# Sparse attention and top-2 experts on one core: how the early expert jobs fetch their rows, how strided values are loaded, and what paces the indirect transfers

## The chip, the cores and the metric

The kernel runs on one core of a Trainium2 chip. The metric is the device time of one execution in microseconds (us); less is better. The time of a kernel is the median over its runs.

The core has five engines that run at the same time and meet through semaphores: TensorE (PE in the profile), which multiplies matrices into PSUM and also transposes; VectorE (DVE); ScalarE (ACT); GpSimd (POOL), which here mostly issues indirect transfers (gathers and scatters whose row numbers lie in SBUF); and SyncE (SP), which issues the plain transfers. Each engine works through its instructions strictly in the order in which they were written.

## The reference

Attention over 8 batches, 8 heads, 576 positions and 64 values per head. Four heads see only the last 32 positions (local), four see only positions with the same remainder by 32 (strided). Its output is x, 4608 tokens of 512 values, and feeds a mixture of 8 experts of which each token uses 2.

```python
def _attn_ref(q, k, v):
    B, H, S, D = q.shape                      # 8, 8, 576, 64
    scores = (1.0 / np.sqrt(D)) * np.matmul(q, k.transpose(0, 1, 3, 2))
    rel = pos[:, None] - pos[None, :]
    mask_local = (rel >= 0) & (rel < 32)
    mask_strided = (rel >= 0) & (pos[None, :] % 32 == pos[:, None] % 32)
    ...                                       # softmax over the masked scores
    return np.matmul(attn, v)

def _moe_ref(x, w_gate, w_noise, noise, w1, w2):   # x: 4608 x 512
    noisy_logits = x @ w_gate + np.log1p(np.exp(x @ w_noise)) * noise
    top2 = np.argpartition(-noisy_logits, 2, axis=1)[:, :2]
    ...                                       # top2_w: softmax over the two
    for e in range(8):
        for k in range(2):
            mask = top2[:, k] == e
            h = np.maximum(x[mask] @ w1[e], 0.0)          # 512 -> 1024
            out[mask] += top2_w[mask, k, None] * (h @ w2[e])  # 1024 -> 512
```

## The kernel before, in words

**Attention.** The work is cut into 32 units: 8 batches times four pairs of heads, strided and local in turn. `loads` (L435) brings a unit's k, q and v through SP two units ahead, `prep` (L476) transposes k and q on PE, `products` (L523) makes the masked scores, `item` (L562) does softmax and values, and `finish` (L648) stores the unit's columns of x to the DRAM tensor `x_dram` and keeps a transposed copy `xT` for the gate. The values of a strided unit go to the tile `v_s`, which keeps 65 numbers per position (64 values and a one), so the load writes 64 values at a time, one line of 256 B each.

**Routing.** After the four units of a batch, `route` (L706) computes the gate for its 576 tokens, ranks the two experts of each, and scatters 12 x 96 entries (token, weight, row of `x_dram`) into `tab`, one list per expert: 12 indirect transfers on POOL per batch (L817).

**Experts.** An expert's list is worked in jobs of two or three blocks of 128 tokens. `SUBS` (L63) gives each job its place in the list and the number `hb` of batches after which those places are certain to be filled. Seven jobs of experts 0 to 2 have `hb` below 8, 16 blocks in all: these early jobs run between the attention units. All others wait for batch 8. For a job, `gather` (L901) loads the entries of the list through SP (L908), makes row numbers on POOL (L935, L954) and gathers the rows of x: `x_dram` holds four 128-column pieces of a token as four rows that lie 576 rows apart, and each block takes four gathers of 128 rows of 512 B (L946), the row numbers being offset by quarter (`qoff`), so that a 32x32 block transposition by DVE (L970, in `transposes`, L960) puts the columns onto the partitions. ACT then rounds the result to a high part (L974) and DVE subtracts it to a low part (L976). `layer1` (L988) and `layer2` (L1049) multiply high and low parts on PE, three products for one, at L1002 and L1064. `previous` (L1037) gathers the rows of the output so far (L1042); they are added on DVE (L1089) and scattered back (L1094). The output is filled with zeros by 12 plain transfers (L1148) of 384 rows each, and `previous` waits for those that cover its batches.

**Order.** Nothing of the order is left to the hardware. Every piece of work is a `Piece` with an engine (ANY is ACT or DVE), an estimated duration, a rank and its dependencies; `issue_all` (L291) is a list scheduler that keeps estimated clocks of all engines and of the wire, takes the piece that can start first (among those within 120 ns the one of lowest rank), and writes its instructions in that order. What the code sets around the change:

- A plain transfer is counted with its bytes times `wires` over 270 bytes per ns; a piece that needs a transfer's data may start `far` ns after its planned landing. A transfer marked `bulk` (a zero fill) is taken only when at most 1500 ns of wire time are planned ahead, and not before its `t0`.
- Expert work on PE is let in by a balance (`owed`) of about one to one with attention, and holds at most four PSUM banks while attention lasts.
- A piece that reads PSUM and writes a ring slot forces the PSUM writer to come after the slot was handed out. So the PE products of a block's layer 2 stand behind the start of `previous` for that block.
- An indirect transfer on POOL is also made to wait for a step of DVE or ACT that is planned to have ended 200 ns before it (the latest of either), so that it doesn't run ahead of its plan:

```python
behind = [x for m in marks.values() for x in m[-40:] if x[0].end + 200 <= t]
if behind:
    x = max(behind, key=lambda x: x[0].end)
    if x[0].end > paced[0]:
        ...   # each transfer y gets: tc.add_manual_dep(y.ins, x[1].ins.name, ...)
paced[0] = t
```

The functions that the diff touches follow, with the profile's line numbers.

Of the kernel before, what the change touches and what calls it, by code (L numbers as in the profile page):

```python
# [22 lines left out]
def kernel(  # L23
# [135 lines left out]
    v_s = [keep.tile([GP, 2, NJ, D + 1], F32, name=f"v_s{i}") for i in range(2)]  # L159
# [131 lines left out]
    def issue_all(expert_banks, t_start):  # L291
# [43 lines left out]
        while ready:  # L335
# [79 lines left out]
    for name, shape, dtype, depth in (  # L415
            ("raw", [LP, 2, LJ, D], F32, 2), ("ord", [LP, LJ, 2, D], F32, 1),
            ("ks", [GP, 2, NJ, D], F32, 1), ("qs", [GP, 2, NJ, D], F32, 1),
            ("mx", [128, 5], F32, 3), ("ex", [128, 5, KW], F32, 2), ("aT", [128, 5, 128], F32, 2),
            ("rs", [128, 6], F32, 2),
            ("xT", [128, S], F32, 6),  # L420
# [14 lines left out]
    def loads(u, rank):  # L435
# [21 lines left out]
        if local:  # L457
# [4 lines left out]
                             [[D, QB], [QB * D, 2 * NBL], [1, D]], 589824)], True)  # L462
# [185 lines left out]
    def finish(u, xo, rank):  # L648
# [3 lines left out]
        base = (b * 4 + d) * S * 128  # L652
# [4 lines left out]
        if local:  # L657
            store(lambda t: t[:, :4, :, :].rearrange("r g h d -> r g (h d)"), 0,
                  [[128, 128], [128 * 128, 4], [1, 128]], 262144)
            store(lambda t: t[:QB, 4, :, :].rearrange("r h d -> r (h d)"), 512 * 128, [[128, QB], [1, 128]], 32768)  # L660
        else:
            for half in range(2):

                store(lambda t, half=half: t[64 * half:64 * half + 64, :4, :, :].rearrange(
                    "r (m g) h d -> r m (g h d)", m=2),
                      (QB + 2 * half) * 128, [[NJ * 128, QB], [4 * 128, 2], [1, 256]], 131072)
            store(lambda t: t[:QB, 4, :, :].rearrange("r h d -> r (h d)"), 0, [[128, QB], [1, 128]], 32768)
# [579 lines left out]
```

## Time and profile before

| | us |
|---|---|
| median of 3 runs | 1115.05 (1113.36 to 1119.16) |
| the profiled execution | 1116.99 |
| its span, first to last instruction | 1115.2 |
| PE busy in the span | 1066.9 (96%) |
| POOL busy | 606.9 (54%) |
| DVE busy | 615.2 (55%) |
| ACT busy | 429.9 (39%) |

The profile is that of one execution. It names instructions by line of the kernel, engine and operation, with `out<-in` tiles; PEld is the weight load of PE, which overlaps the products, and SPq, POOLq are transfers as their engine issues them. PEclk is the share of the full TensorE clock that was granted. A busy PE is not a PE at its peak: at half the clock it is busy twice as long. The attention units fill the span to about 315 us; from about 366 us on the kernel does expert jobs alone.

### The profile page before, as it was taken

What the parts mean: (1) busy time and instruction counts of PE and PEld (TensorE: products, weight loads), DVE (VectorE), ACT (ScalarE), POOL (GpSimd) and SP (SyncE); (2) the same over time, 40 slices, a digit from 0 to 9 for tenths busy, and PEclk for the clock granted to TensorE, in tenths of its full rate; (3) what the DMA queues carried; (4) which work ended last, traced back from release to release, by engine and by line L of the source; (5) the groups of instructions that cost most, each with busy time, mean ns of one, the idle gap of its engine ahead of it and who ended that gap; (6) DMA issues with size and microseconds to landing.
All of it is one profiled execution on the core that took longest, in us unless ns stands there. A gap on an engine that the chain in (4) does not pass through costs nothing.

```text
span 1115.2 us, 23354 instructions
## 1 busy us (share of the span) xinstructions
PE 1066.9 (96%) x8581; PEld 940.5 (84%) x8581; DVE 615.2 (55%) x1618; ACT 429.9 (39%) x1103; POOL 606.9 (54%) x789
## 2 busy tenths in 40 slices
PE   7988889899998999999999999999999999999993
PEld 5767669788887989898998989898988898898992
DVE  4787976867764434655673455345534643473430
ACT  5687966856633211423341223123311321151220
POOL 1044464566656765656666555655646474656510
PEclk6898979999999999999999999999999999999997
DMA  9698997879775532445553226324522452253210
GB/s 189 165 204 199 229 219 172 184 199 248 198 203 102 161 88 72 135 145 148 176 165 117 83 78 195 95 61 115 174 74 68 126 164 69 77 161 92 73 42 22
DMA packets 184886, 153.03 MB, mean 137 GB/s; under 512 B 74695, under 2 KB 155079, under 8 KB 184752
## 3 DMA queue, kind: packets, MB, share of 16 engines
q1 hardware_dynamic: 159664, 92.40, 34.3%
q0 software_dynamic: 25088, 58.87, 17.7%
q8 instruction: 81, 1.33, 0.5%
q14 instruction: 53, 0.43, 0.1%
HBM read 112.86 MB, written 39.39 MB: 137 GB/s over the span
## 4 chain that ended last, share of the span: by engine, by line
PE 66%; DMA 0%; DVE 0%; issue 0%; POOL 0%; POOLq 0%; DVEq 0%
PE bankE L1064 5%; PE bankF L1064 5%; PE bankH L1064 4%; PE bankD L1064 4%; PE bankB L1064 4%; PE bankB L1002 4%; PE bankD L1002 4%; PE bankF L1002 4%; PE bankC L1002 4%; PE bankH L1002 4%; PE bankE L1002 4%; PE bankA L1002 4%; PE bankG L1002 4%; PE bankC L1064 4%; PE bankA L1064 4%; PE bankG L1064 3%
## 5 line engine op out<-in xcount | busy, mean ns | idle before, releaser
L946 POOL DMA_INDIRECT xg<-x_dram,gxx x304 | 307.4, 1011 | 145.0 <-issue 69.9
L1094 POOL DMA_INDIRECT out_dram<-prev,tabt x80 | 83.3, 1041 | 105.0 <-DVE prev L1089 38.5
L817 POOL DMA_INDIRECT tab<-ent,addr x96 | 93.4, 973 | 62.5 <-issue 10.3
L1042 POOL DMA_INDIRECT prev<-out_dram,gix x80 | 78.3, 979 | 80.5 <-DMA out_dram<-prev,tabt 29.4
L970 DVE STREAM_TRANSPOSE xr<-xg 128x512 f32<-128x512 f32 (+1 forms) x80 | 84.3, 1054 | 20.2 <-DMA xg<-x_dram,gxx 18.5
L974 ACT CAST xhi<-xr 128x512 fp32r<-128x512 f32 (+1 forms) x80 | 47.7, 596 | 95.7 <-DVE xr L970 92.7
L976 DVE TENSOR_TENSOR xlo<-xr,xhi 128x512 fp32r<-128x512 f32 (+1 forms) x80 | 53.2, 665 | 26.4 <-ACT xhi L974 25.0
L888 DVE TENSOR_TENSOR w1lo<-wraw,w1hi 128x512 fp32r<-128x512 f32 x80 | 55.0, 690 | 6.6 <-ACT w1hi L887 4.3
L887 ACT CAST w2hi<-wraw 128x512 fp32r<-128x512 f32 x80 | 46.7, 617 | 29.4 <-DMA wraw<-in_moe_w_dram 8.4
L888 DVE TENSOR_TENSOR w2lo<-wraw,w2hi 128x512 fp32r<-128x512 f32 x80 | 52.1, 682 | 3.9 <-ACT w2hi L887 3.3
L887 ACT CAST w1hi<-wraw 128x512 fp32r<-128x512 f32 x80 | 48.6, 614 | 2.5 <-DMA wraw<-in_moe_w_dram 2.4
L1002 PE MATMUL bankB<-xhi,w1hi 128*128 128x256 f32 (+3 forms) x128 | 39.4, 308 | 2.6 <-ACT xhi L974 2.6
L1002 PE MATMUL bankG<-xhi,w1hi 128*128 128x256 f32 (+3 forms) x136 | 41.1, 302 | 0.0
L1002 PE MATMUL bankG<-xhi,w1lo 128*128 128x256 f32 (+3 forms) x136 | 40.7, 300 | 0.0
L1002 PE MATMUL bankG<-xlo,w1hi 128*128 128x256 f32 (+3 forms) x136 | 40.5, 298 | 0.0
L1002 PE MATMUL bankE<-xhi,w1hi 128*128 128x256 f32 (+3 forms) x132 | 39.9, 302 | 0.0
L1002 PE MATMUL bankD<-xhi,w1hi 128*128 128x256 f32 (+3 forms) x132 | 39.8, 302 | 0.0
L1002 PE MATMUL bankC<-xhi,w1hi 128*128 128x256 f32 (+3 forms) x132 | 39.7, 301 | 0.0
L1002 PE MATMUL bankB<-xlo,w1hi 128*128 128x256 f32 (+3 forms) x128 | 38.8, 303 | 0.7 <-DVE xlo L976 0.7
L1002 PE MATMUL bankD<-xhi,w1lo 128*128 128x256 f32 (+3 forms) x132 | 39.4, 298 | 0.0
L1002 PE MATMUL bankC<-xhi,w1lo 128*128 128x256 f32 (+3 forms) x132 | 39.4, 298 | 0.0
L1002 PE MATMUL bankE<-xhi,w1lo 128*128 128x256 f32 (+3 forms) x132 | 39.4, 298 | 0.0
(614 smaller groups left out, 3474.3 us busy)
## 6 DMA issues: line engine op xcount, KB each, us to landing
wraw<-in_moe_w_dram SPq DMA_DIRECT2D x160, 256.0 KB
out_dram<-zeros SPq DMA_DIRECT2D x12, 768.0 KB
xg<-x_dram,gxx POOLq DMA_INDIRECT x304
ks<-in_k_dram SPq DMA_DIRECT2D x15, 320.0 KB
qs<-in_q_dram SPq DMA_DIRECT2D x15, 320.0 KB
v_s<-in_v_dram SPq DMA_DIRECT2D x30, 160.0 KB
raw<-in_k_dram SPq DMA_DIRECT2D x16, 288.0 KB
v_l<-in_v_dram SPq DMA_DIRECT2D x16, 288.0 KB
```

Source lines behind the costliest of these rows:

```text
L817: st = nc.gpsimd.indirect_dma_start(out=tab, out_offset=bass.IndirectOffsetOnAxis(ap=s["addr"].t[:, t, kk:kk + 1], axis=0), in_=s["ent"].t ...
L887: Piece("ACT", act(512) + 30, lambda o: nc.scalar.copy(hi.t, raw.t), rank, read=[raw], alloc=[hi], expert=True)
L888: Piece("DVE", dve(512), lambda o: nc.vector.tensor_tensor(lo.t, raw.t, hi.t.bitcast(F32), ALU.subtract), rank, read=[raw, hi], alloc=[lo] ...
L946: dma(lambda o, i=i, g=g, xg=xg: nc.gpsimd.indirect_dma_start(out=xg.t[:, g, :], out_offset=None, in_=x_dram[:4 * known, :], in_offset=bas ...
L970: Piece("DVE", dve(4 * rows), lambda o, xg=xg, xr=xr, ng=ng, rows=rows: nc.vector.transpose(xr.t[:, :, :rows].rearrange("p c (g i) -> p g ...
L974: Piece("ACT", act(4 * rows), lambda o, xr=xr, rows=rows, cols=cols: nc.scalar.copy(xh.t[:, :, cols], xr.t[:, :, :rows]), rank, read=[xr], ...
L976: Piece("DVE", dve(4 * rows), lambda o, xr=xr, rows=rows, cols=cols: nc.vector.tensor_tensor(xl.t[:, :, cols], xr.t[:, :, :rows], xh.t[:, ...
L1002: nc.tensor.matmul(ps.t[:, :width], a.t[:, 128 * d:128 * d + 128], c.t[:, d, :width], start=(m == 0), stop=(m == len(todo) - 1))
L1042: dma(lambda o: nc.gpsimd.indirect_dma_start(out=pv.t[:rows, :], out_offset=None, in_=out[:known, :], in_offset=bass.IndirectOffsetOnAxis( ...
L1064: nc.tensor.matmul(ps.t, HT[n, f][p[0]].t[:, cols], W2[n][f][p[1]].t, start=(m == 0), stop=(m == len(todo) - 1))
L1094: st = nc.gpsimd.indirect_dma_start(out=out[:known, :], out_offset=bass.IndirectOffsetOnAxis(ap=tb.t[:rows, i, 0:1], axis=0), in_=pv.t[:ro ...
```

## The change

Five things change.

1. **Pacing of indirect transfers.** An indirect transfer on POOL now waits for the latest DVE step that is planned to have ended 200 ns earlier and later than the transfer before it; only if there is none, for such a step of ACT.
2. **List loads.** The plan starts a list load 4000 ns (`far`) after the planned landing of the scatters that it needs, not at once.
3. **Strided values.** A strided unit's values come in two loads (one per head) of 2 KB lines into a new tile `vraw` (one buffer), and ACT or DVE copies each into `v_s`. The plan's cost of loads changes with it: factor 1.65 in place of 1.45 on 256 B lines, 1.2 now on the 1.5 KB lines of local k and q, and local values counted with their true 294,912 B in place of twice as much.
4. **Rows of x.** `x_dram` is laid out by token: the four pieces of a token follow each other, 2 KB in one line. The stores of `finish` and the row numbers follow. An early job then gathers a block with one indirect transfer of 128 whole rows, by the same row numbers that `previous` uses, without the second list load and its row numbers; PE transposes the block in four 128x128 steps into one PSUM bank, from which ACT and DVE take high and low parts. Jobs with `hb` = 8 gather as before, in four, and are transposed on DVE.
5. **Zero fills and room.** The planned starts of the zero fills become 26, 36, 46, 56, 66 and then 111, 121 ... 171 us, from 50, 68 ... 248 us. `xT` has 5 buffers, not 6.

```diff
-    v_s = [keep.tile([GP, 2, NJ, D + 1], F32, name=f"v_s{i}") for i in range(2)]
+    v_s = [keep.tile([G, 2, NJ, D + 1], F32, name=f"v_s{i}") for i in range(2)]
...
-    nc.gpsimd.iota(xrow, pattern=[[4 * S, B], [TB, T]], base=0, channel_multiplier=1)
+    nc.gpsimd.iota(xrow, pattern=[[4 * TB, NTOK // TB]], base=0, channel_multiplier=4)
...
-        nc.vector.memset(qoff[32 * i:32 * i + 32, :], float(i * S))
+        nc.vector.memset(qoff[32 * i:32 * i + 32, :], float(i))
...
             if e == "POOL" and o.lat:
-                behind = [x for m in marks.values() for x in m[-40:] if x[0].end + 200 <= t]
-                if behind:
-                    x = max(behind, key=lambda x: x[0].end)
-                    if x[0].end > paced[0]:
+                for engine in ("DVE", "ACT"):
+                    behind = [x for x in marks[engine][-40:] if paced[0] < x[0].end <= t - 200]
+                    if behind:
+                        x = max(behind, key=lambda x: x[0].end)
                         for y in last if isinstance(last, list) else [last]:
                             tc.add_manual_dep(y.ins, x[1].ins.name, mybir.DependencyInfo(
                                 mybir.DependencyClass.Sync, mybir.DependencyReason.DATA), reason="in its time")
+                        break
                 paced[0] = t
...
-            ("xT", [128, S], F32, 6),
+            ("xT", [128, S], F32, 5),
...
-                    nbytes, rank, wires={D: 1.45, 4 * D: 1.2}.get(dims[-1][1], 1.0),
+                    nbytes, rank, wires={D: 1.65, LJ * D: 1.2}.get(dims[-1][1], 1.0),
...
-                             [[D, QB], [QB * D, 2 * NBL], [1, D]], 589824)], True)
+                             [[D, QB], [QB * D, 2 * NBL], [1, D]], 294912)], True)
...
-            put("v", R["v_s"].new(),
-                [(lambda t, h=h: t[:rows, h, :, :D], v, base + h * S * D, [[NJ * D, rows], [D, NJ], [1, D]], 2048 * rows)
-                 for h in range(2)], True)
+            slot = res["v"] = R["v_s"].new()
+            for h in range(2):
+                put(f"v{h}raw", R["vraw"].new(), [(lambda t: t[:rows].rearrange("p j d -> p (j d)"), v, base + h * S * D,
+                                                   [[NJ * D, rows], [1, NJ * D]], 2048 * rows)], True)
+                def spread(o, h=h, raw=res[f"v{h}raw"]):
+                    copy(o.e, slot.t[:G, h, :, :D], raw.t[:G])
+                Piece("ANY", {"ACT": act(NJ * D), "DVE": 75 + 0.52 * NJ * D}, spread, rank, read=[res[f"v{h}raw"]],
+                      **{"write" if h else "alloc": [slot]})
...
-        base = (b * 4 + d) * S * 128
+        base = b * S * DM + d * 128
...
-                    "r (m g) h d -> r m (g h d)", m=2),
-                      (QB + 2 * half) * 128, [[NJ * 128, QB], [4 * 128, 2], [1, 256]], 131072)
+                    "r (m g) h d -> r m g (h d)", m=2),
+                      (QB + 2 * half) * DM, [[NJ * DM, QB], [4 * DM, 2], [DM, 2], [1, 128]], 131072)
...
+            whole = hb < B
+            tb, gi = R["tabt"].new(), R["gix"].new()
+            tx, gx = (None, None) if whole else (R["tabx"].new(), R["gxx"].new())
...
-                dma(load, bytes_, rank if hb == B else 20 * NP * (hb - 1) + 10 * NP, after=known_tab[hb], expert=True, **how)
+                dma(load, bytes_, rank if hb == B else 20 * NP * (hb - 1) + 10 * NP, after=known_tab[hb], expert=True,
+                    far=4000, **how)
...
+            for i in range(nb) if whole else ():
+                xg = R["xg"].new()
+                dma(lambda o, i=i, xg=xg: nc.gpsimd.indirect_dma_start(
+                    out=xg.t.rearrange("p g c -> p (g c)"), out_offset=None,
+                    in_=x_dram.rearrange("(t q) c -> t (q c)", q=4)[:known, :],
+                    in_offset=bass.IndirectOffsetOnAxis(ap=gi.t[:, i:i + 1], axis=0)),
+                    262144, rank, eng="POOL", read=[gi], after=known_stores[hb], expert=True, alloc=[xg])
+                xs.append(xg)
...
+                if hb < B:
+                    xr = Slot()
+                    def tr(o, xg=xg, xr=xr):
+                        xv = xg.t.rearrange("p g c -> p (g c)").rearrange("p (x c) -> p c x", c=ND)
+                        for c in range(ND):
+                            nc.tensor.transpose(xr.t[:, 128 * c:128 * c + 128], xv[:, c, :], ident)
+                    Piece("PE", 108 * ND, tr, rank, read=[xg], psum=xr, expert=True)
+                else:
+                    xr = R["xr"].new()
+                    Piece("DVE", 8 * rows, lambda o, xg=xg, xr=xr, ng=ng, rows=rows: nc.vector.transpose(
...
-            ER - 1, t0=50000 + 18000 * c, bulk=True))
+            ER - 1, t0=26000 + 10000 * c + 35000 * (c >= 5), bulk=True))
```

More of the change, by code (lines that the diff above doesn't have):

```diff
@@ L863 @@
             ("tabt", [128, 3, 3], I32, 3), ("gix", [128, 3], I32, 3), ("tabx", [128, 12, 3], I32, 2),
[L864 removed]
+            ("gxx", [128, 3, 4], I32, 2), ("xg", [128, 4, 128], F32, 2), ("xr", [128, ND * 128], F32, 1),
             ("xhi", [128, ND, WID], F32R, 1), ("xlo", [128, ND, WID], F32R, 1),
@@ L903, in gather @@
             known = hb * S
-            tb, gi, tx, gx = R["tabt"].new(), R["gix"].new(), R["tabx"].new(), R["gxx"].new()
+            whole = hb < B
+            tb, gi = R["tabt"].new(), R["gix"].new()
+            tx, gx = (None, None) if whole else (R["tabx"].new(), R["gxx"].new())
             def entries(dst, p0, n, how, bytes_, dims):
@@ L916, in load @@
                         early_loads.append((ld, hb))
-                dma(load, bytes_, rank if hb == B else 20 * NP * (hb - 1) + 10 * NP, after=known_tab[hb], expert=True, **how)
-            entries(lambda: tx.t[:, :4 * nb, :].rearrange("p b c -> p (b c)"), start, 128 * nb, {"alloc": [tx]}, 16384,
-                    [[0, 4], [12 * nb, 32], [1, 12 * nb]])
+                dma(load, bytes_, rank if hb == B else 20 * NP * (hb - 1) + 10 * NP, after=known_tab[hb], expert=True,
+                    far=4000, **how)
+            if not whole:
+                entries(lambda: tx.t[:, :4 * nb, :].rearrange("p b c -> p (b c)"), start, 128 * nb, {"alloc": [tx]}, 16384,
+                        [[0, 4], [12 * nb, 32], [1, 12 * nb]])
             ng = tail // 32
@@ L939, in xindices @@
                                             qoff[:, 0:1], op0=ALU.min, op1=ALU.add)
-            Piece("POOL", 360 if tail else 230, xindices, rank, read=[tx] + ([tx2] if tail else []), alloc=[gx],
-                  expert=True)
+            if not whole:
+                Piece("POOL", 360 if tail else 230, xindices, rank, read=[tx] + ([tx2] if tail else []), alloc=[gx],
+                      expert=True)
             xs = []
-            for i in range(nb + (tail > 0)):
+            for i in () if whole else range(nb + (tail > 0)):
                 xg = R["xg"].new()
@@ L965, in transposes @@
             for i in range(nb + (tail > 0)):
-                xg, xr = G_[n][2][i], R["xr"].new()
+                xg = G_[n][2][i]
                 rows = 128 if i < nb else tail
@@ L969, in transposes, with view @@
                 cols = slice(128 * i, 128 * i + rows)
-                Piece("DVE", dve(4 * rows), lambda o, xg=xg, xr=xr, ng=ng, rows=rows: nc.vector.transpose(
-                    xr.t[:, :, :rows].rearrange("p c (g i) -> p g c i", g=ng),
-                    xg.t[:, :ng, :].rearrange("p g (i c) -> p g c i", c=ND)), rank, read=[xg], alloc=[xr], expert=True)
-                how = "write" if i else "alloc"
-                Piece("ACT", act(4 * rows), lambda o, xr=xr, rows=rows, cols=cols: nc.scalar.copy(
-                    xh.t[:, :, cols], xr.t[:, :, :rows]), rank, read=[xr], expert=True, **{how: [xh]})
-                Piece("DVE", dve(4 * rows), lambda o, xr=xr, rows=rows, cols=cols: nc.vector.tensor_tensor(
-                    xl.t[:, :, cols], xr.t[:, :, :rows], xh.t[:, :, cols].bitcast(F32), ALU.subtract),
+                if hb < B:
[8 more added lines that the diff above has]
+                    Piece("DVE", 8 * rows, lambda o, xg=xg, xr=xr, ng=ng, rows=rows: nc.vector.transpose(
+                        xr.t.rearrange("p (c x) -> p c x", c=ND)[:, :, :rows].rearrange("p c (g i) -> p g c i", g=ng),
+                        xg.t[:, :ng, :].rearrange("p g (i c) -> p g c i", c=ND)), rank, read=[xg], alloc=[xr], expert=True)
+                how = "write" if i else "alloc"
+                def view(xr=xr, rows=rows):
+                    return xr.t.rearrange("p (c x) -> p c x", c=ND)[:, :, :rows]
+                Piece("ACT", act(4 * rows), lambda o, view=view, cols=cols: nc.scalar.copy(
+                    xh.t[:, :, cols], view()), rank, read=[xr], expert=True, **{how: [xh]})
+                Piece("DVE", dve(4 * rows), lambda o, view=view, cols=cols: nc.vector.tensor_tensor(
+                    xl.t[:, :, cols], view(), xh.t[:, :, cols].bitcast(F32), ALU.subtract),
                       rank, read=[xr, xh], expert=True, **{how: [xl]})
```

13 lines of the change are left out of this document (6 added, 7 removed).

## Prediction

> **What bounds the kernel now.** I read the page first, then the table by stages, then PE's, POOL's and SP's timelines around the places where PE loses time.
>
> ```profile
> span 1115.2 us, 23354 instructions
> PE 1066.9 (96%) x8581; PEld 940.5 (84%) x8581; DVE 615.2 (55%) x1618; ACT 429.9 (39%) x1103; POOL 606.9 (54%) x789
> PEclk6898979999999999999999999999999999999997
> ```
>
> PE is busy nearly all the time, so the time is PE's work plus what PE loses, by standing idle or by running at a lower granted clock. The table says where.
>
> ```profile
> core 0: us, PE busy (x) PEld busy (x) DVE busy (x) ACT busy (x) POOL busy (x), PEclk, DMA share, GB/s
> 0.00:35.00 35.00, 28.73 (x306) 22.61 (x307) 16.20 (x76) 19.86 (x53) 4.65 (x31) 0.66 0.88 166
> 35.00:90.00 55.00, 49.52 (x848) 40.56 (x846) 44.12 (x197) 41.22 (x131) 13.26 (x29) 0.97 0.93 205
> 90.00:150.00 60.00, 49.43 (x828) 40.04 (x826) 51.27 (x210) 51.45 (x157) 31.69 (x57) 0.94 0.94 212
> 150.00:165.00 15.00, 14.29 (x171) 11.89 (x172) 11.97 (x45) 9.83 (x33) 9.21 (x18) 0.54 1.17 227
> 190.00:220.00 30.00, 26.02 (x449) 21.45 (x448) 25.72 (x109) 24.92 (x78) 17.76 (x33) 0.94 0.95 206
> 220.00:355.00 135.00, 134.47 (x1372) 116.29 (x1371) 90.52 (x317) 70.14 (x195) 85.52 (x132) 1.00 0.76 193
> 355.00:366.00 11.00, 7.75 (x30) 6.47 (x29) 6.61 (x10) 4.15 (x9) 5.69 (x7) 0.84 0.50 151
> 366.00:1100.00 734.00, 732.10 (x4256) 658.94 (x4255) 353.77 (x617) 193.06 (x406) 427.93 (x467) 1.00 0.38 111
> ```
>
> From 366 us on PE loses 1.9 us in 734: nothing done to gathers or waits can shorten that part, it can only lengthen it. 220 to 355 is full too. Three places after 150 us lose time. 150 to 165: 0.7 idle, and the clock at 0.54 costs 14.29 x 0.46 = 6.6, together 7.3. 190 to 220: 4.0 idle and 30 x 0.06 = 1.8 of clock, 5.8. 355 to 366: 3.25 idle and 11 x 0.16 = 1.8, 5.0. Sum 18.1 us. Before 150 us there are 6.3 + 5.5 + 10.6 = 22.4 idle and, by the same product, 35 x 0.34 + 55 x 0.03 + 60 x 0.06 = 17.2 of clock; no expert job can run there, as none has its rows.
>
> **Why PE loses after 150 us.** These rows, from POOL's, SP's and PE's timelines, show expert work arriving late.
>
> ```profile
> 141.24 0.91 POOL L817 DMA_INDIRECT tab<-ent,addr  x1 [0.22 <-issue]
> 144.12 1.06 POOL L946 DMA_INDIRECT xg<-x_dram,gxx  x1 [1.23 <-issue]
> 154.24 0.94 POOL L946 DMA_INDIRECT xg<-x_dram,gxx  x1 [1.10 <-DVE ns L791]
> 156.83 1.07 DVE L970 STREAM_TRANSPOSE xr<-xg 128x512 f32<-128x512 f32 x1
> 164.57 1.11 DVE L970 STREAM_TRANSPOSE xr<-xg 128x512 f32<-128x512 f32 x1
> 167.78 0.36 PE L1002 MATMUL bankB<-xhi,w1hi 128*128 128x256 f32 x1
> 59.98 0.59 SPq L1148 DMA_DIRECT2D out_dram<-zeros  x1
> 186.85 1.48 SPq L1148 DMA_DIRECT2D out_dram<-zeros  x1
> 219.81 0.97 POOL L1042 DMA_INDIRECT prev<-out_dram,gix  x1 [0.30 <-issue]
> 220.19 0.48 PE L1064 MATMUL bankD<-w2hi,hhi 128*128 128x512 f32 x1
> ```
>
> The first job's eight gathers take POOL from 144.12 to 155.2, behind the scatters of batch 2; its second block is transposed on DVE only at 164.57 and PE starts it at 167.78: until then PE has attention alone. Its layer 2 must stand behind `previous`, which waits for three zero fills (1152 rows); the third is issued at 186.85, and then POOL is in the scatters of a batch, so `previous` starts at 219.81 and layer 2 at 220.19. That is the 190 to 220 loss.
>
> ```profile
> 355.67 1.27 POOL L946 DMA_INDIRECT xg<-x_dram,gxx  x1 [0.85 <-ACT xhi L974]
> 359.32 1.08 DVE L970 STREAM_TRANSPOSE xr<-xg 128x512 f32<-128x512 f32 x1 [2.59 <-DMA xg<-x_dram,gxx]
> 360.33 1.25 DVE L888 TENSOR_TENSOR w2lo<-wraw,w2hi 128x512 fp32r<-128x512 f32 x2
> 361.10 0.44 PE L1002 MATMUL bankB<-xhi,w1hi 128*128 128x384 f32 x1 [2.56 <-ACT xhi L974]
> 362.23 0.47 PE L1002 MATMUL bankB<-xlo,w1hi 128*128 128x384 f32 x1 [0.69 <-DVE xlo L976]
> ```
>
> The third loss is the last of twelve gathers of a job, which shares POOL with the scatters of batch 7: it goes out at 355.67, and PE waits 2.56 + 0.69 us for what DVE and ACT make of it.
>
> **The change, part by part.**
>
> ```profile
> L946 POOL DMA_INDIRECT xg<-x_dram,gxx x304 | 307.4, 1011 | 145.0 <-issue 69.9
> L1042 POOL DMA_INDIRECT prev<-out_dram,gix x80 | 78.3, 979 | 80.5 <-DMA out_dram<-prev,tabt 29.4
> L970 DVE STREAM_TRANSPOSE xr<-xg 128x512 f32<-128x512 f32 (+1 forms) x80 | 84.3, 1054 | 20.2 <-DMA xg<-x_dram,gxx 18.5
> 76.79 0.66 PE L681 MATMUL bankC<-ident,xo 128*128 128x128 f32 x4
> 77.28 0.38 PE L590 MATMUL bankG<-ident,ex 128*72 128x128 f32 x2
> 157.06 0.58 ACT L283 COPY aT<-bankD 96x512 f32<-96x512 f32 x1
> L974 ACT CAST xhi<-xr 128x512 fp32r<-128x512 f32 (+1 forms) x80 | 47.7, 596 | 95.7 <-DVE xr L970 92.7
> L681 PE MATMUL bankD<-ident,xo x24: 270/273/474, 87.3 to 269.1; 128*128 128x128 f32 x24
> ```
>
> *Whole rows.* 16 blocks lose 64 gathers of 1.011 us and get 16 that are `previous`'s kind of transfer (128 rows of 2 KB, 0.979 us): 64.7 - 15.7 = 49 us of POOL, none of it on PE's path as such. What PE gains is the place. The first job's last gather goes out at about 144.1 + 1.4 (the spacing of the eight, 10.12 / 7) = 145.5, not 154.2. PE can then start some 9 us earlier, at about 159; without DVE's queue ahead of the transposition (156.8 to 164.6 for two blocks) nearer to 153. I take two thirds of the 7.3 us back, 4.9; the ends are 0 and 7.3. At 355 three transfers stand where twelve did, 9 x 1.27 = 11.4 us less of POOL, against a gap of 3.25: all 5.0 go. Next late would be the parts of the new weights, which DVE still makes at 360.33; layer 2 needs them only after layer 1's 96 products.
>
> *PE transposes.* 64 new steps. Four of the same shape (L681) start at 76.79 and the next group starts at 77.28: 0.49 us for four, 64 x 0.1225 = 7.8 us. After 150 us PE has no idle room left if the rest holds, so all of it lies on the path: +7.8. The new source is read with a step of four elements, which no row shows; the ends are 0 (all in gaps) and 64 x 273 ns = 17.5 (each alone).
> The Trainium skill (TensorE: Matmul & The Clock Gate, Part 4: PE-mode transpose) gives about 275 ns for one in a kernel; taken per step that would be 17.6 us. The rows agree with its number as a duration, and show that four in a row overlap.
> DVE loses 16 x 1.054 = 16.9 us; off PE's path, taken as 0. ACT's high part now comes out of PSUM: a copy of 512 from there (aT) takes 0.58 us, its cast from SBUF 0.596, so nothing changes. The transposed block takes one of the four PSUM banks that expert work may hold; these are handed on within a few us, 0.
>
> *Zero fills.* The three that the first job needs are planned from 26 us, ahead of the expert weights. Then `previous` can go right behind the gathers and layer 2 behind layer 1, which fills 190 to 220: 5.3 of the 5.8 us back; ends 0 and 5.8.
>
> ```profile
> L286 DVE COPY ord<-raw x6: 541/546/700, 45.0 to 248.1; 96x768 f32<-96x768 f32 x6
> v_s<-in_v_dram SPq DMA_DIRECT2D x30, 160.0 KB
> q1 hardware_dynamic: 159664, 92.40, 34.3%
> PE bankC L501 <- DMA qs<-in_q_dram: 0.5, 1, 0.5
> DVE xr L970 <- issue: 0.4, 1, 0.4
> ```
>
> *Long lines.* 32 loads now need 2,544 lines of 2 KB instead of 20,352 of 256 B. A packet of this queue takes 0.343 x 1115.2 x 16 / 159,664 = 38 ns of one engine, so up to 17,808 x 38 / 16 = 43 us of wire are freed, by bytes nothing. PE waits for loads hardly at all (0.5 us in that row), and the zero fills moved forward take room in the same stage: 0. The price is 32 copies of 512 elements, 0.546 x 512/768 = 0.36 on DVE to 0.60 on ACT, some 18 before 150 us: 6.5 to 10.8 us on two engines that are 75 to 85% busy there. If half an engine's share reached PE it would be 5.4; if all fall into idle time, 0. I take +1.0. `vraw` has one buffer, so SP's second load waits for the first copy, and SP's next loads and stores queue behind it; units are loaded two ahead, so 0.
>
> *The waits.* POOL's transfers wait for a DVE step more often than for ACT's; behind a waiting one stand POOL's scatters and gathers, and for those wait the lists and now PE. The list load planned 4 us later, `xT`'s fifth buffer and the shorter x stores: 0 each, as POOL and SP have idle time.
>
> Sum: -4.9 - 5.0 + 7.8 - 5.3 + 1.0 = -6.4. The span becomes 1108.8, the profiled execution (1116.99, 1.8 above its span) 1110.6. The median of the runs lies 1.94 below that execution: 1115.05 - 6.4 = **1108.6 us**.
>
> **Rivals.**
> *Nothing comes of it (15%).* A zero fill is taken only when the planned wire is short: before, the one planned at 86 us went out at 186.85. If that holds, the 5.3 stay lost: -1.1, 1114. For it: DMA shares of 0.88 to 0.94 before 150 us. Against: the plan's wire becomes lighter (local values count half). With transposes at 273 ns each the sum is +3.3, 1118, the other way to no change.
> *A late gather stops PE (20%), slower.* Before, DVE stood in line for the rows; now PE does, in order, and everything behind it. A stall like that at 358 costs 5.0 with its clock. 16 blocks can each make one; two turn the sum to +3.6, three give +8.6, 1123.7. For it: POOL waits on DVE's real progress (1.10 at 154.24). Against: in DVE's waits before 330 us (the last row above) it stood only 0.4 us before L970, and not for a transfer.
> The Trainium skill (SBUF - State Buffer, "SBUF: two separate sides", the "DVE blocks DMA" note) says that an fp32 copy on DVE locks GpSimd out of writing descriptors; it speaks for this rival through the 32 copies. The copy row's 700 ns against 546 is no proof of it.
> *More than forecast (15%).* With all 18.1 back and half of the 14.2 lost between 90 and 150 (10.6 idle, 3.6 clock) too, it is 7.8 - 18.1 - 7.1 = -17.4, 1097.7.
>
> **How the numbers follow.** A measurement of this kernel can tell about 0.5%, 5.6 us, from no change. The forecast has 50%. Its own range goes from all three losses back and the copies at nothing, 7.8 - 18.1 = -10.3, to nothing back at 150 us, 7.8 - 5.0 - 5.3 + 1.0 = -1.5: 1104.8 to 1113.6, and I put 0.30 of the 0.50 beyond -5.6. Faster: 0.30 + 0.15 = 0.45. Slower: 0.18 of the late gather's 0.20. The rest, 0.37, is within 0.5%. Cases of both signs are in play, so the range reaches to about where three late gathers and the larger gain end: 1097 to 1123.
>
> **What would show it.** Right: first L1002 before 160 us, clock 1.00 soon after 155; the third zero fill before 100 us, first L1064 before 200; no PE gap over 1 us between 160 and the last stage; PE transposes at 0.49 us per four. Wrong: PE waiting for `xg` by DMA; zero fills still after 150 us; unit spacing before 150 us over the present; or any idle PE after 370 us.

## The result, and the profile after

The changed kernel takes 1106.5 us in the median (1102.82 to 1110.57, 9 runs), the kernel before beside it 1115.05 (1112.88 to 1119.16, 9 runs): a ratio of 0.9909, 95% interval 0.9888 to 0.9930, 8.55 us less. Forecast were 1108.6 and 6.4 less. The profiled execution took 1104.51 us with a span of 1102.8, against 1116.99 and 1115.2.

The page of the kernel after:

```profile
span 1102.8 us, 23359 instructions
PE 1064.4 (97%) x8645; PEld 938.3 (85%) x8645; DVE 607.6 (55%) x1606; ACT 432.8 (39%) x1131; POOL 553.8 (50%) x734
PEclk8999999999899999999999999999999999999998
```

POOL has 53.1 us less to do, about the 49 that were worked out. PE's clock line begins at 8 in place of 6, has fewer dips up to the sixth slice, and a new one in the eleventh (276 to 303 us). The same table by stages as before, with the end cut off at the last product:

```profile
core 0: us, PE busy (x) PEld busy (x) DVE busy (x) ACT busy (x) POOL busy (x), PEclk, DMA share, GB/s
0.00:35.00 35.00, 30.65 (x417) 24.42 (x417) 24.09 (x99) 21.85 (x66) 4.62 (x31) 0.90 0.84 182
35.00:90.00 55.00, 47.99 (x813) 38.86 (x813) 44.40 (x196) 42.40 (x138) 14.37 (x31) 0.94 0.96 226
90.00:150.00 60.00, 51.74 (x861) 40.61 (x860) 55.88 (x221) 55.35 (x175) 33.32 (x59) 1.00 1.07 236
150.00:165.00 15.00, 14.70 (x226) 12.61 (x226) 10.32 (x29) 11.30 (x39) 7.52 (x15) 0.89 1.05 227
190.00:220.00 30.00, 29.99 (x370) 26.36 (x369) 22.11 (x64) 18.89 (x57) 15.71 (x27) 1.00 0.87 214
220.00:355.00 135.00, 128.78 (x1363) 110.72 (x1362) 84.22 (x306) 74.54 (x209) 50.19 (x86) 0.96 0.61 162
355.00:366.00 11.00, 11.00 (x62) 10.68 (x61) 5.50 (x10) 3.84 (x8) 6.83 (x15) 1.00 0.67 187
366.00:1090.00 724.00, 724.00 (x4231) 651.68 (x4230) 343.91 (x607) 190.35 (x400) 411.73 (x457) 1.00 0.37 111
```

Read as a ledger (idle time, plus the stretch's length times the missing clock; in the row 150 to 165, as in the prediction, PE's busy time times the missing clock), PE's losses before and after are:

| stretch, us | before | after | change |
|---|---|---|---|
| 0 to 35 | 18.2 | 7.9 | -10.3 |
| 35 to 90 | 7.1 | 10.3 | +3.2 |
| 90 to 150 | 14.2 | 8.3 | -5.9 |
| 150 to 165 | 7.3 | 1.9 | -5.4 |
| 165 to 220 | 6.2 | 0.0 | -6.2 |
| 220 to 355 | 0.5 | 11.6 | +11.1 |
| 355 to 366 | 5.0 | 0.0 | -5.0 |
| PE's last product to the end | 17.1 | 12.3 | -4.8 |

Together -23.3. The new transpositions add 8.5 (below), which makes -14.8; the span fell by 12.4. The ledger closes to 2.4 us: the ends of PE's instructions are modelled, and the granted clock comes in steps of 3.4 us. Between other runs it closes less well: for the kernel with the zero fills late again (below) its rows give 12.4 us more than after where the span is 4.3 longer, so a single row is good to a few us only. And the 12.4 us are those of two executions, the one before 1.9 us above its median, the one after 2.0 below; between the medians it is 8.55. The four rows from 150 to 366 us were in the prediction, with their sizes or as a rival. Those before 150 us were there only as half of a rival, and the last one not at all.

The rows that answer to those of the prediction come from PE's, POOL's and SP's timelines of the kernel after:

```profile
135.52 0.92 POOL L824 DMA_INDIRECT tab<-ent,addr  x1 [0.21 <-issue]
138.01 1.41 POOL L973 DMA_INDIRECT xg<-x_dram,gix  x1 [0.40 <-POOL gix L967]
139.72 0.95 POOL L973 DMA_INDIRECT xg<-x_dram,gix  x1 [0.30 <-issue]
158.76 0.36 PE L1037 MATMUL bankA<-xhi,w1hi 128*128 128x256 f32 x1
46.42 0.62 SPq L1183 DMA_DIRECT2D out_dram<-zeros  x1
66.36 1.23 SPq L1183 DMA_DIRECT2D out_dram<-zeros  x1
160.60 0.58 SPq L1183 DMA_DIRECT2D out_dram<-zeros  x1
181.80 0.48 PE L1099 MATMUL bankF<-w2hi,hhi 128*128 128x512 f32 x1
```

The first job's rows come in two transfers, the last at 139.72, not in eight up to 154.24. They still stand behind batch 2's scatters, whose last is at 135.52 now and was at 141.24: of the 14.5 us that the last gather gained, 6.1 are an earlier start (138.01 for 144.12) and 8.4 the fewer gathers. Layer 1 starts at 158.76 (before: 167.78), layer 2 at 181.80 (before: 220.19). But the third zero fill still goes out only at 160.60.

PE's waits from 155 us on, and what stands behind the two large ones:

```profile
PE bankF L550 <- DVE prev L1124: 3.7, 1, 3.7
PE bankC L998 <- DMA xg<-x_dram,gix: 2.3, 1, 2.3
```

```profile
234.79 0.20 POOL L812 COPY ent<-wt 96x12 f32<-96x12 f32 x1 [0.80 <-DVE wt L806]
276.63 0.97 POOL L973 DMA_INDIRECT xg<-x_dram,gix  x1 [41.65 <-PE bankD L998]
277.91 0.93 POOL L824 DMA_INDIRECT tab<-ent,addr  x1 [0.21 <-POOL spacer L823]
291.33 0.91 POOL L824 DMA_INDIRECT tab<-ent,addr  x1 [0.21 <-issue]
297.41 1.00 POOL L1077 DMA_INDIRECT prev<-out_dram,gix  x1 [2.54 <-DMA out_dram<-prev,tabt]
```

This is the loss between 220 and 355 us, in five rows. POOL has the weights of batch 5 ready at 234.79, and next in its queue is the whole gather of a job's third block. `xg` has two buffers, so that gather needs the first block to have been transposed by PE, and PE has that transposition behind the layer 1 of the job before. POOL stands for 41.65 us; when it may go on, twelve scatters and two output scatters stand in front of the first `previous` of the job before, which starts at 297.41; that job's layer 2 has run since 276.12. PE waits 2.3 us for the third block's rows, and 3.7 for a PSUM bank (`bankF`) that DVE can clear only when `previous` has landed.

### The profile page after: what moved, and what is told of

It reads as the page before. It is cut to its first block, busy times and chain, and to the rows that moved or that the text cites. A ratio compares the mean times of both kernels' runs of the same rounds, so it can differ in the third digit from the quotient of the medians.

```text
span 1102.8 us, 23359 instructions
## 1 busy us (share of the span) xinstructions
PE 1064.4 (97%) x8645; PEld 938.3 (85%) x8645; DVE 607.6 (55%) x1606; ACT 432.8 (39%) x1131; POOL 553.8 (50%) x734
## 4 chain that ended last, share of the span: by engine, by line
PE 82%; DVE 5%; issue 5%; DMA 4%; ACT 3%; POOL 0%; POOLq 0%; DVEq 0%; SPq 0%
PE bankE L1099 5%; PE bankF L1099 5%; PE bankG L1099 5%; PE bankC L1099 5%; PE bankG L1037 5%; PE bankF L1037 5%; PE bankA L1099 5%; PE bankH L1037 5%; PE bankC L1037 5%; PE bankA L1037 5%; PE bankD L1099 4%; PE bankB L1037 4%; PE bankD L1037 4%; PE bankE L1037 4%; PE bankH L1099 4%
## 5 line engine op out<-in xcount | busy, mean ns | idle before, releaser
L959 POOL DMA_INDIRECT xg<-x_dram,gxx x240 | 241.4, 1006 | 105.1 <-issue 55.7
L1002 DVE STREAM_TRANSPOSE xr<-xg 128x512 f32<-128x512 f32 (+1 forms) x64 | 66.3, 1037 | 12.7 <-DMA xg<-x_dram,gxx 11.2
L1011 DVE TENSOR_TENSOR xlo<-xr,xhi 128x512 fp32r<-128x512 f32 (+1 forms) x64 | 42.1, 658 | 18.4 <-ACT xhi L1009 17.2
L973 POOL DMA_INDIRECT xg<-x_dram,gix x16 | 16.8, 1050 | 58.4 <-PE bankD L998 42.8
L1056 ACT ACTIVATE hhi<-bankG 128x256 fp32r<-128x256 f32 (+2 forms) x34 | 14.3, 421 | 70.9 <-PE bankG L1037 70.9
L1037 PE MATMUL bankG<-xhi,w1lo 128*128 128x256 f32 (+3 forms) x136 | 40.3, 296 | 0.0
L1037 PE MATMUL bankF<-xhi,w1hi 128*128 128x256 f32 (+3 forms) x132 | 39.9, 302 | 0.0
L1037 PE MATMUL bankH<-xhi,w1hi 128*128 128x256 f32 (+3 forms) x132 | 39.7, 301 | 0.0
L1037 PE MATMUL bankA<-xhi,w1hi 128*128 128x256 f32 (+3 forms) x132 | 39.6, 300 | 0.0
L1037 PE MATMUL bankF<-xhi,w1lo 128*128 128x256 f32 (+3 forms) x132 | 39.4, 298 | 0.0
L1037 PE MATMUL bankF<-xlo,w1hi 128*128 128x256 f32 (+3 forms) x132 | 39.3, 298 | 0.0
```

Source lines behind the costliest of these rows:

```text
L959: dma(lambda o, i=i, g=g, xg=xg: nc.gpsimd.indirect_dma_start(out=xg.t[:, g, :], out_offset=None, in_=x_dram[:4 * known, :], in_offset=bas ...
L973: dma(lambda o, i=i, xg=xg: nc.gpsimd.indirect_dma_start(out=xg.t.rearrange("p g c -> p (g c)"), out_offset=None, in_=x_dram.rearrange("(t ...
L1002: Piece("DVE", 8 * rows, lambda o, xg=xg, xr=xr, ng=ng, rows=rows: nc.vector.transpose(xr.t.rearrange("p (c x) -> p c x", c=ND)[:, :, :row ...
L1011: Piece("DVE", dve(4 * rows), lambda o, view=view, cols=cols: nc.vector.tensor_tensor(xl.t[:, :, cols], view(), xh.t[:, :, cols].bitcast(F ...
L1037: nc.tensor.matmul(ps.t[:, :width], a.t[:, 128 * d:128 * d + 128], c.t[:, d, :width], start=(m == 0), stop=(m == len(todo) - 1))
```

## The experiments

**How the groups compare.** The first four kernels ran on a chip where the kernel before took 1113.6 us, much as for the result. The other eight ran in two groups of four on two other chips (numbers 6 and 14; the first is 0). On both of these the kernel before took 1180 us, and every profile has waits that the trace gives to no step of the kernel: 30 to 69 us on ACT and 62 to 109 on DVE, where the profiles of the first chip have at most 3.7 and 8. There only ratios within a group are read. Taken from ratios, the kernel after is at 0.9909 for the result and 0.9816 (0.9772 to 0.9861) on chip 14. One caution holds for all that follows: a part taken back also changes the plan elsewhere, so a run shows what the kernel does without the part, not the part's price alone.

**The zero fills late again.**

```
-            ER - 1, t0=26000 + 10000 * c + 35000 * (c >= 5), bulk=True))
+            ER - 1, t0=50000 + 18000 * c, bulk=True))
```

> The kernel after with one part undone: the zero fills are planned from 50 us on, 18 us apart, as before. My theory: the first job's layer 2 waits behind the fills again, so 190 to 220 us loses about the 5.8 us that it lost before: the time is the kernel after's 1106.5 plus 5 to 6, about 1112, and the first layer-2 product is near 215 to 220 us in place of 181.8. Rival: the fills come early anyhow, because the local values and the queue's new order freed the plan's wire: third fill before 150 us, time 1106.5 within 2.

Measured: 1106.44 us, ratio 0.9923 (0.9893 to 0.9953), the same as the kernel after. My theory fell, and the rival fell in its particular too, as the third fill goes out at 176.81, not before 150:

```profile
176.81 0.60 SPq L1183 DMA_DIRECT2D out_dram<-zeros  x1
184.45 0.97 POOL L1077 DMA_INDIRECT prev<-out_dram,gix  x1 [8.18 <-DMA out_dram<-zeros]
185.17 0.48 PE L1099 MATMUL bankD<-w2hi,hhi 128*128 128x512 f32 x1
190.00:220.00 30.00, 29.99 (x460) 25.15 (x453) 24.54 (x79) 21.70 (x66) 17.06 (x30) 1.00 0.97 235
```

A fill at 176.81 holds up `previous` (the second row's 8.18 us), and layer 2 still starts at 185.17 with nothing lost from 190 to 220. So the moved fills are not what won that stretch. Before, the fill at 186.85 was followed by 33 us until `previous` ran at 219.81, because POOL first had the next job's eight gathers to finish (the last at 197.89) and then a batch of scatters (the last at 218.59); here it is free to go within 8. The run also has the rows come when the prediction had them, from 144.30 to 145.86, and layer 1 starts at 162.98.

**The transpositions on PE done twice.**

```
-                        for c in range(ND):
+                        for c in (*range(ND), *range(ND)):
                             nc.tensor.transpose(xr.t[:, 128 * c:128 * c + 128], xv[:, c, :], ident)
```

> The kernel after, where each of the 16 early blocks' four transpositions on TensorE is done twice into the same place (64 more steps, same result). My theory (they lie on PE's path at 0.12 us each): +7.8 us, about 1114. Rival 1 (they fit into PE's gaps): within 2 of 1106.5. Rival 2 (each costs a full 273 ns): +17.5, about 1124.

Measured: 1112.3 us, ratio 0.9988 (0.9969 to 1.0008): 5.8 us over the kernel after by medians, 8.8 by ratios. From one block's timeline of the kernel after (four) and of this one (eight):

```profile
275.61 0.75 PE L998 MATMUL bankD<-ident,xg 128*128 128x128 f32 x4
276.12 0.48 PE L1099 MATMUL bankF<-w2hi,hhi 128*128 128x512 f32 x1
```

```profile
189.57 1.14 PE L998 MATMUL bankA<-ident,xg 128*128 128x128 f32 x8
190.54 0.27 PE L598 MATMUL bankG<-ident,ex 128*96 128x128 f32 x1
```

From the start of a block's transpositions to the next instruction's it is 0.51 us for four and 0.97 for eight; over all 16 blocks 8.5 us after and 16.7 here. They lie on PE's path and cost 0.13 us each (0.09 to 0.14 by the times). Neither rival holds.

**Unit 1's loads ahead of unit 2's, on the kernel before.** These are SP's first loads in the kernel before, and in the one after:

```profile
1.73 0.73 SPq L443 DMA_DIRECT2D v_s<-in_v_dram  x1
5.57 0.60 SPq L443 DMA_DIRECT2D v_s<-in_v_dram  x1
7.38 0.43 SPq L443 DMA_DIRECT2D raw<-in_k_dram  x1
```

```profile
1.73 0.44 SPq L445 DMA_DIRECT2D vraw<-in_v_dram  x1
3.65 0.59 SPq L445 DMA_DIRECT2D raw<-in_k_dram  x1
7.82 0.39 SPq L445 DMA_DIRECT2D vraw<-in_v_dram  x1
```

`vraw` has one buffer, so unit 2's values (7.82) can't go ahead of unit 1's keys any more, which are asked for at 3.65 in place of 7.38. Unit 1's scores start at 15.77 in place of 22.57. The experiment makes that order without the long lines:

```
-    LL = {0: loads(0, 0), 1: loads(1, 10)}
+    LL = {0: loads(0, 0), 1: loads(1, 5)}
```

> The kernel before with one number changed: the loads of unit 1 get rank 5 in place of 10, so that they stand ahead of unit 2's (rank 6) in SP's queue, as they stand in the kernel after, where the one buffer of the long values holds unit 2's back. No long lines, no whole rows. Theory 1 (the gain of 10.3 us before 35 us came from the order of the loads): unit 1's scores start near 16 us in place of 22.6, the clock's half-speed stretch of 24 us at the start shrinks to under 10, and the time falls by 8 to 10 us from 1115, to 1105 to 1107. Theory 2 (it came from the shorter transfers of the long lines): unit 1's scores stay at 20 us or later and the time is 1115 within 3.

Measured: 1123.63 us, ratio 1.0067 (1.0040 to 1.0094): slower. Its first three stages:

```profile
0.00:35.00 35.00, 30.04 (x439) 23.90 (x441) 26.38 (x106) 24.19 (x71) 4.64 (x31) 0.95 1.01 205
35.00:90.00 55.00, 48.08 (x787) 39.04 (x785) 42.35 (x184) 40.95 (x131) 18.88 (x39) 0.86 0.93 205
90.00:150.00 60.00, 55.23 (x784) 44.79 (x785) 45.14 (x173) 45.67 (x142) 27.89 (x49) 0.79 0.90 203
```

The first half of theory 1 holds: unit 1 starts at 15.9 us, the clock is 0.95, and the first 35 us lose 6.7 in place of 18.2. The second half does not: 35 to 150 us lose 32.0 in place of 21.3, and it is all given back. The order of the loads makes the better start, but here that start is worth nothing at 150 us.

**The third whole gather planned behind the transposition that frees its buffer.**

```
-            for i in range(nb) if whole else ():
+            for i in range(min(nb, 2)) if whole else ():
...
             for i in range(nb + (tail > 0)):          # in transposes()
+                if hb < B and i >= 2:
+                    whole_rows(n, i, rank - 2)
```

`whole_rows` is the old loop's body, made a function.

> The kernel after, where the whole-row gather of a third block of an early job is planned only when the first block's transposition, which frees its buffer, has been planned. My theory: in the three-block job POOL no longer stands 41.65 us in front of that gather, the scatters of the next batch go out in time, and the 11.6 us that PE lost between 220 and 355 us (idle 6.2, clock 5) mostly go: 1106.5 minus 8 to 10, about 1097. Rival: POOL's place is taken by another late step, since PE's transpositions still stand behind the previous job's layer 1 and the third gather then comes later: gaps of the same size a few tens of us on, 1106.5 within 3.

Measured: 1095.62 us (1093.10 to 1096.31), ratio 0.9827 (0.9803 to 0.9850), the fastest on this chip, below the kernel after by 10.9 us by medians and 9.1 by ratios. Its stage, and the gather in question:

```profile
220.00:355.00 135.00, 134.59 (x1443) 117.60 (x1442) 89.94 (x321) 79.44 (x222) 57.53 (x99) 1.00 0.67 181
241.71 0.95 POOL L824 DMA_INDIRECT tab<-ent,addr  x1 [4.73 <-issue]
279.20 0.94 POOL L979 DMA_INDIRECT xg<-x_dram,gix  x1 [4.55 <-PE bankG L1005]
```

The gather goes out no earlier (279.20), but batch 5's scatters now stand in front of it and start at 241.71, not 277.91. The loss in this stage falls from 11.6 to 0.4 us. The rival, a gap of the same size further on, does not show. So the plan's blindness to one buffer cost 9 to 11 us. The stop is in every profile of a kernel with whole rows gathered as in the kernel after, on all three chips: POOL stands there for 37 to 42 us. With the third gather planned later it never waits over 5 us for PE there.

**One part alone, and all but one part** (chip 6). Two questions were left: whether whole rows or long lines carry the gain, and what either does alone. The first kernel is the one before with whole rows alone, the second the one before with long lines alone, the third the one after with four-piece gathers (`whole = False`, DVE transposing), the fourth the one after with short lines:

```
-            slot = res["v"] = R["v_s"].new()
-            ...                      # two long loads into vraw, a copy of each
+            put("v", R["v_s"].new(),
+                [(lambda t, h=h: t[:G, h, :, :D], v, base + h * S * D, [[NJ * D, G], [D, NJ], [1, D]], 2048 * G)
+                 for h in range(2)], True)
```

> The kernel before with the whole-row gathers alone: x stored row by row, early blocks gathered whole, transposed on TensorE. Strided values short, zero fills, list loads, wire weights and POOL's waits as before. Theory: the losses at 150, 190 and 355 us go (7.3, 5.8 and 5.0 before), since rows come earlier, with the fills where they were; the 64 transpositions cost 7.8, and a third whole gather may stop PE between 220 and 355 us as in the kernel after (11.1). 1115 - 18.1 + 7.8 = 1104.7 without the stop, 1115.8 with it; the first 35 us stay as before (PE's clock 0.66). Rival (the first part of the gain needs the early zero fills): layer 2 is late again, a loss of 5 to 6 us at 190 to 220, 1110 to 1121.

> The kernel before with the long lines of the strided values alone (one buffer of long values, a copy for each half; xT one buffer less to make room). Theory 1 (the long lines bring the start's gain and keep it to 150 us, as the loads take less wire): PE's clock over the first 35 us near 0.9, first expert product before 162 us, the time 8 to 12 us below before, 1103 to 1107. Theory 2 (any gain at the start is given back by 150 us as with the loads' order alone, DVE and ACT having 32 copies more): unit 15 starts at 130 us or later, the time 1113 to 1122.

> The kernel after with early jobs' rows gathered in four pieces and transposed on DVE again (x in its new order in memory, everything else kept). Theory: by PE's ledger 7.8 of transpositions and some 10 of the 11.6 us lost between 220 and 355 go, but the waits for rows at 150, 190 and 355 us come back (5.4, 5.8, 5.0 gained before): 1106.5 - 17.8 + 16.2, about 1105; POOL is busy some 50 us more. Rival 1 (whole rows carry the gain): 1112 or more. Rival 2 (the losses at 150 and 190 us had gone through the earlier start, not through whole rows): only the 5.0 at 355 comes back, about 1094.

> The kernel after with the strided values loaded in short lines straight into place (unit 2's loads go ahead of unit 1's again). Theory (the long lines bring the gain before 150 us): unit 1's scores start after 20 us in place of 15.8, PE's clock over the first 35 us falls to about 0.7, and the time rises by 8 to 13 us, to 1115 to 1119. Rival (the 32 copies cost what the start gains): 1106.5 within 3.

Measured, against 1180 us before: 0.9967 (0.9937 to 0.9996), 0.9971 (0.9934 to 1.0008), 0.9973 (0.9937 to 1.0009) and 0.9825 (0.9780 to 0.9870). As the kernel after had not run in that group, it was run in another, on chip 14, with the last two again:

> The kernel after unchanged, as the measure beside the next three: before took 1114 in one group of runs and 1180 in another, so each is read against the kernel before and this one in its own group. Expected: 0.991 of before, as first measured.

> The kernel after with early jobs' rows in four pieces and DVE transposing again, repeated: in the group where before took 1180 it was 0.9973 of before. Theory (by PE's ledger, as put there: 17.8 us of transpositions and late third gather saved, 16.2 of waits come back): within 4 us of the kernel after. Rival 1 (whole rows carry the gain): 6 us or more slower than after, the losses at 150 to 165, 190 to 220 and 355 us all back. Rival 2 (the losses at 150 and 190 us went through the earlier start): 8 to 12 us faster than after.

> The kernel after with short lines for the strided values, repeated: 0.9825 of before in the other group, where after was not run. Theory (long lines bring the gain before 150 us): PE's clock over the first 35 us about 0.7 in place of 0.90, 8 to 13 us slower than after. Rival (the start's gain is given back by 150 us, or the 32 copies cost as much as it brings): within 3 us of after, or faster.

Measured: the kernel after 0.9816 (0.9772 to 0.9861), four pieces 0.9975 (0.9953 to 0.9997), short lines 0.9835 (0.9793 to 0.9877). For the four pieces rival 1 holds: without whole rows nearly all of the gain is gone, 21.6 us in that group, of which 4.8 lie behind PE's last product (last section). My ledger had it even, and fell. Two stages of the kernel after in that group, then of the one with four pieces, with the last gather but one of its first job and the start of its layer 1:

```profile
150.00:220.00 70.00, 67.03 (x812) 57.72 (x812) 47.34 (x197) 42.29 (x137) 29.06 (x52) 0.88 0.79 201
355.00:440.00 85.00, 84.42 (x569) 75.22 (x569) 39.26 (x109) 26.35 (x62) 37.29 (x57) 1.00 0.42 119
```

```profile
150.00:220.00 70.00, 59.96 (x830) 49.42 (x823) 46.56 (x203) 45.79 (x141) 34.49 (x62) 0.85 0.71 171
355.00:440.00 85.00, 78.14 (x434) 68.19 (x434) 42.11 (x103) 24.84 (x54) 52.73 (x69) 0.96 0.42 114
194.53 0.97 POOL L959 DMA_INDIRECT xg<-x_dram,gxx  x1 [1.50 <-DVE aT L286]
211.25 0.36 PE L1037 MATMUL bankB<-xhi,w1hi 128*128 128x256 f32 x1
```

PE idles 3.0 and 0.6 us in these two stages with whole rows, 10.0 and 6.9 with four pieces. Expert work is late again, as the prediction described it, but not at its places. The first job's last two gathers of eight (194.53 and 195.81) now stand behind batch 3's scatters (170.68 to 192.11), so that layer 1 starts at 211.25 where the kernel after has 179.57. PE idles little more from 150 to 165 (2.3 us for 1.4) and from 355 to 366 (0.8 for 0.0), but much more from 165 to 220 (7.7 for 1.6) and from 366 to 440 (6.1 for 0.6).

For the long lines the theory fell and the rival's time holds, though not its cause: short lines cost 2.9 us of 1155.6 by medians, with intervals that overlap, and what the copies cost was not taken apart. Unit 1's scores start later (21.36 us for 16.40), and the clock over the first 35 us does fall, to 0.66 here against 0.78 for the kernel after:

```profile
0.00:35.00 35.00, 30.32 (x321) 24.43 (x322) 19.52 (x81) 18.44 (x54) 4.60 (x31) 0.66 0.94 191
```

Again a worse start, and no loss at the end. The two kernels with one part alone decide little. With long lines alone the time lies between the two theories' ranges, nearer the second, and layer 1 starts at 220.49, not before 162. With whole rows alone it lies between the theory's two cases and inside the rival's range, and not all three losses go: the stop at the third gather is there (POOL stands 38.94 us), PE's longest wait behind it is 14.7 us, and from 355 to 366 it idles 9.8 of 11 us. And the parts don't add up: whole rows alone take 0.3% off, long lines alone 0.3%, all together 1.8%; whole rows with everything but the long lines 1.7% (chips 6 and 14, on which the two kernels that ran on both agree within 0.1%). Between the kernel with whole rows alone (0.9967) and the one with everything but long lines (0.9835) lie POOL's waits for DVE, the list loads' 4 us, the wire weights, one `xT` buffer and the zero fills. Of these only the fills were tried by themselves, and there (first chip) they were worth nothing. What POOL's new waits and the later list loads are worth was never tried: they are a rival for the rest of the gain that these runs leave standing.

**Both repairs together.** Third gather as above, short lines, and unit 1's loads ranked ahead (the edits shown before).

> The kernel after with the third whole gather planned behind the first block's transposition (0.9827 of before alone), and besides with short lines and unit 1's loads ranked ahead of unit 2's, so that the order of the loads is the one of after without its long lines and copies. If the order alone carries the start's gain: 0.980 to 0.984 of before, clock over the first 35 us 0.85 or more, and held to 150 us. If the lighter wire is what holds it: the gain at the start is given back between 35 and 150 us, as with the order alone on the kernel before, and it is 0.988 to 0.995 of before.

Measured: 1143.02 us where before took 1180.49, 0.9702 (0.9663 to 0.9741), below both ranges. The bounds were set from the first chip, so it is read against the kernel after in its group: 0.9702 / 0.9816 = 0.988; the third gather alone made 0.9827 / 0.9909 = 0.992 on the first chip. The clock over the first 35 us is 0.90. By the ledger it loses 8.3 us there and 40.3 up to 150 us; the kernel after in this group loses 12.6 and 43.4, the one with short lines and the old order 16.6 and 44.2. So without the long lines nothing is lost when the order of the loads is kept, though of 8.3 us won at the start against the old order only 3.9 are left at 150. The two repairs stand together; whether this kernel beats the third gather alone is open, as the two didn't run on one chip.

## Why the prediction was right, and where it wasn't

The time came within 2.1 us, and faster, as forecast. The terms behind it fared unevenly, and that the sum came so near is in part luck.

- *The first loss at 150 us, -4.9:* measured -5.4. Layer 1 starts at 158.76, "before 160 us", and the clock is 0.57 from 150 to 154 and 1.00 from then to 165, as "soon after 155" had it. The mechanism given, fewer gathers, is there, but that the start came as forecast is luck: 6.1 us of the earlier rows are the lead from before 150 us, which the forecast did not have. In the kernel with the zero fills late again, whose rows come at the forecast time, layer 1 starts at 162.98 and the row loses 4.9.
- *355 us, -5.0:* measured -5.0; PE does not idle there.
- *PE's transpositions, +7.8:* measured +8.5, at 0.53 us per four in place of 0.49, and doubling them showed that they are on the path. The read step of four elements costs next to nothing. The 17.5 us for transpositions that each take their whole duration did not happen, and so not the Trainium skill's figure (TensorE: Matmul & The Clock Gate, Part 4: PE-mode transpose; its 128x128 there is bf16) taken per step either; as a duration it still agrees with the trace, where the median of one is 285 ns in the largest group:

```profile
L998 PE MATMUL bankB<-ident,xg x16: 271/285/386, 194.1 to 373.8; 128*128 128x128 f32 x16
```

- *Zero fills, -5.3:* the size came true (5.8), the cause did not. The step said that the fills would go early and so free `previous`. The third went out at 160.60, as the rival "nothing comes of it" had it, and with the old times the kernel is as fast. What freed `previous` is that POOL was in neither the next job's gathers nor a batch's scatters when the fill landed. That whole rows do this is not shown: with four pieces `previous` goes out at 197.47, 9.4 us behind the third fill, and it is layer 1 that is late. Fewer gathers, POOL's new waits and the earlier start were not separated.
- *Long lines, +1.0:* the term stands within what can be measured (0 to -3 us), but its working missed the main thing. That `vraw` has one buffer was set at 0 because "units are loaded two ahead". It changed the order of SP's first loads, and with it the first 35 us by 10.3 us.
- *The gain before 150 us, 13.0 us, not forecast.* "More than forecast" had 7.1 of it, between 90 and 150 us, and gave no reason for it. The first 35 us are shown to be the order of the loads: changing it alone makes the better start, and short lines lose it unless the order is kept. Why the lead lasts to 150 us in the kernel after, and was given back when the order alone was changed, is open.
- *A late gather stops PE, the rival at 20%, priced at 5.0 a stall:* it came true in one place, twice over, with 11.1 us, beside the forecast rather than in its stead. The prediction had its form (POOL in order behind a transfer, and PE behind it) but looked for it in DVE's waits. It was to be found in the code: a ring of two buffers, jobs of three blocks, and a gather planned before the step that frees its buffer exists.
- *The end, -4.8, not forecast.* The row 366 to 1100 was read as 1.9 us of PE's loss. That is the time behind PE's last product at 1098.1; PE lost nothing there, and the stretch behind it was not read at all. That "nothing done to gathers or waits can shorten that part" is wrong for it: what shrank is the closing of POOL's indirect transfers, with 48 fewer of them (last section).

The forecast of 6.4 thus came out near 8.55 because two things that it did not know (13.0 and 4.8 gained) were somewhat larger than a stall that it held for unlikely (11.1); errors of 17.8 and 11.1 us happened to offset each other. Two of the signs named for a wrong forecast appeared (PE waiting for `xg`, and a zero fill after 150 us), and a sign for a right one, no PE gap over 1 us after 160, did not; they told the truth about those steps, not about the sum.

The rival's helper, the Trainium skill's "DVE blocks DMA" note (SBUF - State Buffer, "SBUF: two separate sides"), could not be seen. The group of DVE's copies in the kernel after:

```profile
L286 DVE COPY v_s<-vraw 72x512 f32<-72x512 f32 x12 | 5.0, 413 | 1.1 <-DMA vraw<-in_v_dram 1.0
```

DVE makes 12 of the 32, 413 ns each, and leaving all 32 out changed nothing that can be measured.

## What to carry to other kernels

A planner that orders the queues is only as good as the waits it knows: where a transfer needs a buffer whose release is planned later, the engine that issues it stands still with all that is behind it, so look for rings that are shorter than the job. Price a change by stage as idle time plus missing clock, and undo its parts one at a time, since here one of four right-sized terms had another cause than the one given and another was met in part by a lead that nobody had forecast. And read the stretch after the last product too.

## What the runs showed of the hardware

**The end of the program takes longer with more indirect transfers.** After the last instruction of the kernel proper, POOL closes its transfers. In the kernel before (560 indirect transfers), from the lines of the branch and of the program's end:

```profile
L1175 POOLq INC_SWDGE_SEM  x1: 2418/2418/2418, 1102.8 to 1102.8; - x1
L1243 POOLq DRAIN  x3: 40/107/9147, 1105.2 to 1115.0; - x3
```

and in the kernel after (512):

```profile
L1210 POOLq INC_SWDGE_SEM  x1: 1492/1492/1492, 1095.1 to 1095.1; - x1
L1278 POOLq DRAIN  x3: 40/107/5390, 1096.6 to 1102.5; - x3
```

Together 11.57 and 6.88 us: 4.7 us for 48 transfers, 98 ns each between these two counts. In all fourteen profiles, on all three chips, the long drain takes 9.1 to 9.2 us with 560 transfers and 5.39 with 512, whatever else differs. No other engine has anything left to do then, so it is all in the time. Two counts don't show that it grows in a straight line, nor whether it goes by transfers or by the rows that they move, since both fell together.

**A short idle time of PE is followed by half the clock.** In the kernel after PE falls idle at 279.2 us for 2.3, and the records show the granted clock at half from 283.6 to 287.0; it falls idle at 298.0 for 3.7, and the clock is at half from 300.7 to 307.5, beginning before PE goes on. Of the 11.6 us lost in that stage 6.2 are idle time and 5.4 clock. With the third gather planned later both idle times are gone, and the clock from 220 to 355 us is 1.00.
